# Eight one-bank PSUM tiles, tanh by single banks, and new prices for changes of tile size in a planned attention and MLP kernel

## The chip, the cores and the metric

The kernel runs on one core of a Trainium2 chip. The metric is the device time of one execution in microseconds (us). The engines are named as in the profile: PE (TensorE matmul) and PEld (its weight loads), DVE (VectorE), ACT (ScalarE), POOL (GpSimd) and SP (the queue that issues the DMAs). Each engine works through its own instructions in the order in which the program lists them.

## The reference

Attention with a soft cap, a first MLP with a rational activation, and a second MLP whose hidden layer is a maximum over three products:

```python
scores = cap * np.tanh(scale * np.matmul(q, k.transpose(0, 1, 3, 2)) / cap)   # 2 x 12 heads, 448 x 448
scores = scores - np.max(scores, axis=-1, keepdims=True)
attn = np.exp(scores); attn = attn / (np.sum(attn, axis=-1, keepdims=True) + 1e-09)
x = heads_joined(np.matmul(attn, v))                      # 896 tokens x 768
h = x @ moe_w_in                                          # 896 x 2048
g = (a0 + a1*h + a2*h**2 + a3*h**3) / (1 + |b0|*|h| + |b1|*h**2 + 1e-6)
x2 = g @ moe_w_out                                        # 896 x 768
h3 = np.maximum(np.maximum(x2 @ w1, x2 @ w2), x2 @ w3)
out = h3 @ w_out2                                         # 896 x 768
```

## The kernel before

**A planner writes the order.** Every piece of work is added as an operation with its engines and their prices (`add`). Then `Flow.issue` plays the whole program through with those prices and emits the instructions of every engine in the order in which the play started them. For PE it takes the operation that is due first; but if that one has another tile size (`mode`) than the one before, it looks for one of the same size that is due at most `SAME` = 3.0 us later. A change of tile size costs `SWITCH` = 0.1 us in the play. The prices decide the order and which engine does work that several can do; on the chip nothing waits for them.

**PSUM.** There are eight banks, allocated as four tiles of two banks (`twos`, L315). The planner hands out single banks (`place`): scores ("sc") take both banks of a pair, (0,1) or (2,3), in the first four groups also (6,7); sums of attention ("av") take bank 4 or 5; the products of the first MLP's upper half ("h") take 6 or 7. When all scores are done, any bank goes to "h" and to the six accumulators "acc" of the lower half. `bank(val)` returns half of a tile, `pair(val)` a whole one. The waits between engines are made from the tiles that the instructions read and write.

**Attention** (about the first 95 to 115 us). In six groups of two head pairs, `scores` makes 42 tiles of 128 x 896: two matmuls side by side on half the rows of the array (L515, mode "rows", 36 tiles) or four quarter ones (L522, "both", 6 tiles). ACT then does one tanh over both banks (`soft`, L535) and one exp (L538). `weighted` multiplies with v (L574, "halves"; the rest L555, "both"), `summed` adds up the exponentials (L597, "quarters"). All of them are fp32 and are priced 0.752 us each (`FULL`). The row sums travel through DRAM (L606 to L632).

**First MLP.** `up` makes 32 units of 18 matmuls, in three parts of six (L663, 0.203 us each by plan). Each unit's bank is read by ACT in `cubic` (L683) and `absolute` (L680) and by DVE in `first` (L694) and `second` (L697). DVE and ACT then form the rational function (L702 to L728) and its two parts (`parts`, L742, L745). `down` multiplies those with the output weights into the accumulators (L770), in two halves of the columns. L770 takes its operands from L742, L745 and the weights, not from L680 to L697.

**Second MLP and output.** `branches` makes 36 products of 18 matmuls (L861), DVE and ACT take the maximum and split it into two parts (`H3`, one column range for each half of the tokens). `output` multiplies seven tiles of 128 tokens (L920) and writes them out. In the plan each output waits for both halves of the tokens of all six H3.

The weights arrive as 64-bit floats; DVE, ACT and POOL decode them (L400 to L441) all along the first two thirds.

Of the kernel before, what the change touches and what calls it, by code (L numbers as in the profile page):

```python
# [8 lines left out]
F32 = mybir.dt.float32  # L9
# [3 lines left out]
AF = mybir.ActivationFunctionType  # L13
# [4 lines left out]
B, H, S, D = 2, 12, 448, 64  # L18
P = 128
# [15 lines left out]
NFULL = S // P  # L35
# [6 lines left out]

BACKLOG = 14.0, 2.0

SWITCH, SAME = 0.1, 3.0
MM, MO, FULL = 0.203, 0.1733, 0.752

SHARE = 0.5
# [22 lines left out]
class Flow:  # L71
# [83 lines left out]
    def issue(self):  # L155
# [12 lines left out]
        mode = None  # L168
# [7 lines left out]
        while left:  # L176
# [4 lines left out]
            while moved:  # L181
                moved = False
                for e in names:
                    if busy[e] > t + 1e-9:
                        continue
                    blocked = set()
                    ahead = dict.fromkeys(names, 0.0)
                    choice = None
                    for op in ready:
                        if choice and (op.due > choice.due + SAME or "pe" not in op.engines or op.mode != mode):  # L190
                            continue
                        first = next(iter(op.engines))
                        cost = op.engines[first]
                        if op.ready > t + 1e-9:
                            continue
                        lacking = {v.kind for v in op.vals if v.at is None}
                        if lacking & blocked:
                            continue
                        ok = op.due - v0 < op.ahead and self.fits(op, v0)
                        if not ok:  # L200
                            if op.due - v0 < min(op.ahead, 14.0):
                                blocked |= lacking
                            continue
                        if e not in op.engines:
                            ahead[first] += cost
                            continue
                        if op.shared and e == "dve" and busy["pool"] > t + 1e-9:
                            continue
                        if e == "sp" and op.due - v0 > BACKLOG[0] and wire > t + BACKLOG[1]:
                            continue  # L210
                        if e == "pool" and not self.port(t, op, ready, busy, current, v0):
                            continue
                        if e != first and op.engines[e] > max(0.0, busy[first] - t) + ahead[first] + cost:
                            ahead[first] += cost
                            continue
                        if e == "pe" and SAME and op.mode != mode:
                            choice = choice or op
                            continue
                        choice = op
                        break  # L220
                    if choice is None:
                        continue
                    op = choice
                    ready.remove(op)
                    for v in op.vals:
                        if v.at is None:
                            self.take(v)
                    dur = op.engines[e]
                    if e == "pe":
                        dur += SWITCH if mode != op.mode else 0.0  # L230
                        mode = op.mode
                    op.on = e
                    current[e] = op
                    busy[e] = t + dur
                    if e == "sp":
                        wire = max(wire, t + 1.0) + op.size / 0.28
                        end = max(wire + 0.6, t + 2.5 + op.size / 0.5)
                    else:
                        end = t + dur + self.TAIL[e]
                    op.done = end  # L240
                    op.fn(e)
                    left -= 1
                    self.log.append((t, busy[e], e, op))
                    for x in (busy[e], end):
                        seq += 1
                        heapq.heappush(events, (x, seq, op if x == end else None))
                        if busy[e] == end:
                            break
                    moved = True
                    if e == "pe":  # L250
                        while head < len(order) and order[head].done is not None:
                            head += 1
                        v0 = order[head].due if head < len(order) else self.clock
# [37 lines left out]
def attention_moe(ctx: ExitStack, tc: tile.TileContext, qk, v, w_in, w_out, w123, w_out2, par, out):  # L291
# [20 lines left out]
    ones = cp.tile([P, 3, Q], F32, name="ones")  # L312
    raws = [sp.tile([P, DM, 2], I32, name=f"raw{i}") for i in range(NRAW)]
    rows = [sp.tile([P, S], F32, name=f"row{i}") for i in range(NROW)]
    twos = [pp.tile([P, 2, 512], F32, name=f"b{i}") for i in range(4)]  # L315
    a0, a1, a2, a3 = (con[:, i : i + 1] for i in range(4))
    b0, b1 = absb[:, 0:1], absb[:, 1:2]
    cap = con[:, CAP : CAP + 1]
# [11 lines left out]
    def two(val):  # L330
        return val.tile
# [2 lines left out]
        return two(val).rearrange("p a s -> p (a s)")[:, :n]  # L334

    def bank(val):
        return twos[val.at[0] // 2][:, val.at[0] % 2]

    def pair(val):
        return twos[val.at[0] // 2]  # L340

    def dma(out_, in_, after=(), vals=(), size=0.0, issue=0.4, **kw):
        return add({"sp": issue}, lambda e: nc.sync.dma_start(out=out_(), in_=in_()), after, vals, size=size, **kw)
# [159 lines left out]
    def scores(d, i):  # L503
        whole_ = i < 2 * NFULL
        r, n = divmod(i, NFULL)
        pis = [2 * d + r] if whole_ else [2 * d, 2 * d + 1]
        t, x = Val("sc", f"sc{d}_{i}"), slot(f"e{d}_{i}")
        t.early = d < EARLY

        def products(e):  # L510
            raw = QK[pis[0]][0]
            q, k = two(raw)[:, 0], two(raw)[:, 1, n * P : n * P + P]
            for j in range(2):
                rr = slice(j * D, j * D + D)
                pe.matmul(pair(t)[:, j, :S], k[rr], q[rr], start=True, stop=True)  # L515

        def ends(e):
            for h, pi in enumerate(pis):
                raw = QK[pi][0]
                for j in range(2):  # L520
                    rr = slice(j * D, j * D + D)
                    pe.matmul(  # L522
                        pair(t)[h * D : h * D + D, j, :S], two(raw)[rr, 1, NFULL * P :], two(raw)[rr, 0],
                        start=True, stop=True,
                    )

        done = add(
            {"pe": FULL}, products if whole_ else ends, [QK[pi][1] for pi in pis], [QK[pi][0] for pi in pis] + [t],
            mode="rows" if whole_ else "both",
        )  # L530
        for th in last_tanh[-2:]:
            th.before(done)

        def soft(e):
            act.activation(two(x), pair(t)[:, :, :S], AF.Tanh, scale=qscale)  # L535

        def expo(e):
            act.activation(two(x), two(x), AF.Exp, scale=cap)  # L538

        th = add({"act": 0.89}, soft, [done, scale_in], [t, x])  # L540
        last_tanh.append(th)
        E[d, i] = x, add({"act": 0.935}, expo, [th], [x])

# [360 lines left out]
    def output(t):  # L904
        tk = slice(t * P, t * P + P)
        ob = slot(f"ob{t}")
        last = t == NT // P - 1
        copies = []
        for half in range(2):
            o = Val("h", f"o{t}_{half}")  # L910
            ck = slice(half * NH, half * NH + NH)

            def products(e, o=o, ck=ck):
                terms = []
                for oc in range(NCC):
                    hi, lo = (flat(H3[oc][z], NT)[:, tk] for z in range(2))
                    wh, wl = w_hl(weights["o2", oc])
                    terms += [(hi, wh[:, ck]), (hi, wl[:, ck]), (lo, wh[:, ck])]
                for i, (h_, w_) in enumerate(terms):
                    pe.matmul(bank(o)[:, :NH], h_, w_, start=i == 0, stop=i == len(terms) - 1)  # L920

            ws = [weights["o2", oc] for oc in range(NCC)]
            done = add(
                {"pe": 18 * MO}, products, [w.done for w in ws] + [d for h in H3 for d in h[2]],
                [o] + [x for w in ws for x in (w.hi, w.lo)] + [x for h in H3 for x in h[:2]],
            )
            first = "dve" if half == 0 else "act"
            cost = {"dve": 0.48, "act": 0.38}
            copies.append(add(
                {first: cost.pop(first), **cost},  # L930
                lambda e, o=o, half=half: copy_on[e](two(ob)[:, half, :NH], bank(o)[:, :NH]), [done], [o, ob],
                due=fl.clock,
            ))
            if last:
                dma(lambda ck=ck: out[tk, ck], lambda half=half: two(ob)[:, half, :NH], [copies[-1]], [ob],
                    size=0.2, issue=0.4, due=fl.clock)
# [54 lines left out]
```

## Time and profile before

| what | value |
|---|---|
| median of 3 runs | 537.22 us (536.57 to 540.04) |
| profiled execution | 537.27 us |
| its span, first to last instruction | 535.5 us |
| busy share of the span | PE 96%, PEld 76%, DVE 66%, ACT 56%, POOL 10% |
| mean granted TensorE clock | 0.996 of 2.4 GHz |

The profiled execution lies 0.05 us above the median. A row of the timeline gives start, length, engine, line, operation and count, and in brackets the idle time of the engine before it with the instruction that ended it. Matmuls are pipelined: their recorded lengths overlap the next one's start, so PE is busy in the record for a while after it has nothing left to start.

### The profile page before, as it was taken

Reading aid. Unit: us, or ns where it says so; the run is one execution under the profiler, and the core shown is the slowest. Engines: PE = TensorE matmul, PEld = TensorE weight load, DVE = VectorE, ACT = ScalarE, POOL = GpSimd, SP = SyncE. Lnnn points to the kernel's source line nnn. Section 1 sums busy time; section 2 is a strip of 40 time slices with the busy share of each in tenths; the row PEclk is TensorE's granted clock in tenths of the full one; section 3 lists DMA queues with packets and bytes.
Section 4 is the critical chain, followed back from the end, with each engine's and each line's share of the span. In section 5 each row is a group of like instructions: output and inputs, shape, how many; then the busy total and the mean of one; then the engine's idle time right before and its main releaser. Section 6 shows DMA issues by size and latency. Waiting matters only on the chain.

```text
span 535.5 us, 6669 instructions
## 1 busy us (share of the span) xinstructions
PE 516.2 (96%) x2637; PEld 409.5 (76%) x2637; DVE 354.7 (66%) x485; ACT 299.1 (56%) x376; POOL 51.6 (10%) x46
## 2 busy tenths in 40 slices
PE   8999999889988999999999999999999999999997
PEld 4223223349777989888888799999999999999997
DVE  0268798699789999986789999989964235311000
ACT  6999899567587767665676853556521220101111
POOL 0121201030223212001000200100000000000000
PEclk9999999899999999999999999999999999999999
DMA  8856635533610003300001578666700000000121
GB/s 311 347 183 215 225 118 210 158 94 117 207 67 2 0 1 118 119 1 1 1 1 59 171 239 263 219 229 235 236 0 1 0 2 0 1 0 2 60 82 66
DMA packets 16448, 58.37 MB, mean 109 GB/s; under 512 B 3592, under 2 KB 6944, under 8 KB 16416
## 3 DMA queue, kind: packets, MB, share of 16 engines
q1 hardware_dynamic: 16416, 57.94, 31.5%
q8 instruction: 20, 0.33, 0.3%
q14 instruction: 12, 0.10, 0.1%
HBM read 55.10 MB, written 2.84 MB: 108 GB/s over the span
## 4 chain that ended last, share of the span: by engine, by line
PE 73%; DVE 14%; ACT 6%; DMA 3%; issue 2%; SPq 1%; DVEq 0%; ACTq 0%
PE b L861 25%; PE b L770 17%; PE b L663 10%; PE b L920 8%; PE b L515 5%; PE b L597 3%; PE b L574 3%; DVE W L697 2%; DMA row<-rsum 2%; DVE T L722 1%; ACT A L680 1%; DVE W L694 1%; DVE W L725 1%; ACT W L683 1%; DVE T L702 1%
## 5 line engine op out<-in xcount | busy, mean ns | idle before, releaser
L861 PE MATMUL b<-x,whm 128*128 128x448 f32 x432 | 122.7, 365 | 0.0
L663 PE MATMUL b<-x,whin 128*128 128x448 f32 x384 | 111.5, 372 | 5.2 <-DVE W L697 5.0
L663 PEld LDWEIGHTS b<-x,whin 128*128 128x128 f32 x384 | 71.2, 189 | 21.0 <-DVE W L697 7.3
L861 PEld LDWEIGHTS b<-x,whm 128*128 128x128 f32 x432 | 81.1, 188 | 6.4
L861 PE MATMUL b<-x,wlm 128*128 128x448 f32 x216 | 78.9, 365 | 0.0
L663 PE MATMUL b<-x,wlin 128*128 128x448 f32 x192 | 70.6, 368 | 0.0
L535 ACT ACTIVATE e<-b,qscale 128x896 f32<-128x896 f32 x42 | 41.3, 1023 | 5.3 <-PE b L515 5.0
L861 PEld LDWEIGHTS b<-x,wlm 128*128 128x128 f32 x216 | 40.6, 188 | 3.2
L538 ACT ACTIVATE e<-e,con 128x896 f32<-128x896 f32 x42 | 42.1, 1053 | 0.0
L770 PE MATMUL b<-gh,whoa 128*128 128x448 f32 x96 | 36.5, 380 | 5.3 <-ACT W L683 1.9
L663 PEld LDWEIGHTS b<-x,wlin 128*128 128x128 f32 x192 | 36.2, 189 | 3.1
L889 ACT CAST h3h<-t 128x448 fp32r<-128x448 f32 x11 | 6.2, 567 | 57.2 <-DVE t L884 57.2
L770 PE MATMUL b<-gh,whob 128*128 128x448 f32 x96 | 35.3, 367 | 1.1 <-DVE x L789 1.1
L770 PE MATMUL b<-gl,whoa 128*128 128x448 f32 x96 | 35.2, 367 | 0.9 <-DVE gl L745 0.9
L683 ACT ACTIVATE W<-b,con 128x448 f32<-128x448 f32 x32 | 23.0, 724 | 22.0 <-PE b L663 19.7
L770 PE MATMUL b<-gh,wloa 128*128 128x448 f32 x96 | 35.1, 366 | 0.0
L770 PE MATMUL b<-gh,wlob 128*128 128x448 f32 x96 | 35.1, 365 | 0.0
L770 PE MATMUL b<-gl,whob 128*128 128x448 f32 x96 | 35.0, 365 | 0.0
L515 PE MATMUL b<-qk 64*128 64x448 f32 x144 | 34.4, 577 | 0.0
L422 ACT ACTIVATE raw<-raw 128x768 uint8<-128x768 uint8 x16 | 31.5, 1972 | 2.0 <-POOL deco L402 1.7
L879 DVE TENSOR_TENSOR t<-b,t 128x448 f32<-128x448 f32 x12 | 7.5, 624 | 36.2 <-PE b L861 23.3
L574 PE MATMUL b<-e,v 128*64 128x448 f32 x144 | 29.8, 548 | 0.0
(115 smaller groups left out, 907.1 us busy)
## 6 DMA issues: line engine op xcount, KB each, us to landing
raw<-in_w_out_dram SPq DMA_DIRECT2D x22, 768.0 KB, 4.8
raw<-in_w_dram SPq DMA_DIRECT2D x18, 768.0 KB, 4.6
raw<-in_w_in_dram SPq DMA_DIRECT2D x16, 768.0 KB, 6.6
qk<-in_qk_dram SPq DMA_DIRECT2D x12, 448.0 KB, 7.9
v<-in_v_dram SPq DMA_DIRECT2D x6, 448.0 KB
row<-rsum SPq DMA_DIRECT2D x24, 112.0 KB, 3.1
out_dram<-ob SPq DMA_DIRECT2D x6, 384.0 KB, 2.7
out_dram<-ob SPq DMA_DIRECT2D x2, 192.0 KB, 1.9
```

Source lines behind the costliest of these rows:

```text
L422: act.activation(byte[:, 4::8], byte[:, 3::8], AF.Copy, scale=1 / 32, bias=-31 / 64)
L515: pe.matmul(pair(t)[:, j, :S], k[rr], q[rr], start=True, stop=True)
L535: act.activation(two(x), pair(t)[:, :, :S], AF.Tanh, scale=qscale)
L538: act.activation(two(x), two(x), AF.Exp, scale=cap)
L574: pe.matmul(bank(o)[j * D : j * D + D, :S], whole(vr, n, r, j), two(x)[:, j], start=False, stop=n == NFULL - 1,)
L597: pe.matmul(bank(t)[g, :S], ones[:, 0 if n < NFULL else 1 + r], two(xs[r][0])[:, j], start=n == 0, stop=n == NFULL, tile_position=(0, (2 * ...
L663: pe.matmul(bank(h)[:, :S], w_, x_, start=cc == 0 and i == 0, stop=cc == NCC - 1 and i == len(terms) - 1)
L683: act.activation(two(w_)[:, i], bank(h)[:, :S], AF.Identity, bias=a2, scale=a3)
L697: dve.scalar_tensor_tensor(out=two(w_)[:, i], in0=two(w_)[:, i], scalar=a1, in1=bank(h)[:, :S], op0=ALU.add, op1=ALU.mult)
L770: pe.matmul(bank(a)[:, :S], w_, g_, start=count[half, o, b] == 1, stop=count[half, o, b] == 3 * NFC)
L861: pe.matmul(bank(o)[:, :S], w_, x_, start=cc == 0 and i == 0, stop=cc == NCC - 1 and i == 2)
L920: pe.matmul(bank(o)[:, :NH], h_, w_, start=i == 0, stop=i == len(terms) - 1)
```

## The change

- The four PSUM tiles of two banks become eight tiles of one bank; `bank` and `pair` follow. The planner's choice of banks stays.
- The tanh over two banks becomes two instructions of 448 columns, one for each bank. Its price in the plan goes from 0.89 to 0.87 us for both.
- The price of a change of tile size goes from 0.1 us to one by the new size: 0.21 "rows", 0.16 "both" and "halves", 0.13 "quarters", 0.2 for full size.
- An output waits in the plan for the halves of the tokens that it reads instead of both. Six of seven tiles lie in one half (384 to 511 lies in both).

```diff
-SWITCH, SAME = 0.1, 3.0
+SWITCH, SAME = {"rows": 0.21, "both": 0.16, "halves": 0.16, "quarters": 0.13, None: 0.2}, 3.0
...
-                        dur += SWITCH if mode != op.mode else 0.0
+                        dur += SWITCH[op.mode] if mode != op.mode else 0.0
...
-    twos = [pp.tile([P, 2, 512], F32, name=f"b{i}") for i in range(4)]
+    singles = [pp.tile([P, 512], F32, name=f"b{i}") for i in range(8)]
...
     def bank(val):
-        return twos[val.at[0] // 2][:, val.at[0] % 2]
-
-    def pair(val):
-        return twos[val.at[0] // 2]
+        return singles[val.at[0]]
+
+    def pair(val, j):
+        return singles[val.at[j]]
...
-                pe.matmul(pair(t)[:, j, :S], k[rr], q[rr], start=True, stop=True)
+                pe.matmul(pair(t, j)[:, :S], k[rr], q[rr], start=True, stop=True)
...
         def soft(e):
-            act.activation(two(x), pair(t)[:, :, :S], AF.Tanh, scale=qscale)
+            for j in range(2):
+                act.activation(two(x)[:, j], pair(t, j)[:, :S], AF.Tanh, scale=qscale)
...
-        th = add({"act": 0.89}, soft, [done, scale_in], [t, x])
+        th = add({"act": 0.87}, soft, [done, scale_in], [t, x])
...
+        halves = range(t * P // S, ((t + 1) * P - 1) // S + 1)
...
-                {"pe": 18 * MO}, products, [w.done for w in ws] + [d for h in H3 for d in h[2]],
+                {"pe": 18 * MO}, products, [w.done for w in ws] + [h[2][b] for h in H3 for b in halves],
```

## Rows read from the trace of the kernel before

**Rows 1.** Busy us (instructions) of each engine by stage; then clock, DMA share, GB/s

```profile
5.00:47.00 42.00, 42.00 (x247) 12.11 (x248) 18.76 (x24) 39.98 (x45) 6.03 (x6) 1.00 0.75 290
47.00:95.00 48.00, 46.15 (x278) 15.37 (x276) 40.25 (x63) 44.60 (x50) 6.57 (x7) 1.00 0.57 187
...
95.00:165.00 70.00, 63.54 (x315) 47.18 (x312) 58.88 (x84) 45.93 (x61) 14.82 (x11) 0.98 0.37 118
165.00:301.00 136.00, 130.31 (x624) 115.42 (x622) 120.38 (x154) 94.94 (x128) 17.48 (x10) 1.00 0.12 38
```

**Rows 2.** Pieces of the chain that ended last: start, us, what

```profile
35.41 3.16 PE b L574 x16
...
41.31 0.95 PE b L515 x4
42.27 0.89 PE b L597 x8
...
90.61 1.42 PE b L663 x6
...
356.92 131.33 PE b L861 x648
488.25 43.73 PE b L920 x252
```

**Rows 3.** PE's waits from 90 to 165: total us, times, longest

```profile
PE b L663 <- DVE W L697: 5.0, 3, 2.0
```

**Rows 4.** PE's waits from 165 to 301

```profile
PE b L770 <- ACT W L683: 1.9, 4, 0.8
PE b L770 <- ACT A L680: 1.4, 1, 1.4
PE b L770 <- DVE W L697: 1.2, 2, 0.7
PE b L770 <- DVE W L694: 0.4, 2, 0.2
```

**Rows 5.** Timeline of PE and of ACT around 223 us

```profile
222.47 0.36 PE L770 MATMUL b<-gh,wloa 128*128 128x448 f32 x1
223.67 0.47 PE L770 MATMUL b<-gh,whoa 128*128 128x448 f32 x1 [0.83 <-ACT W L683]
...
222.90 0.72 ACT L683 ACTIVATE W<-b,con 128x448 f32<-128x448 f32 x1
224.58 0.55 ACT L680 ACTIVATE A<-b 128x448 f32<-128x448 f32 x1 [0.97 <-PE b L770]
```

**Rows 6.** Timeline of all engines, 115 to 122 us

```profile
115.63 0.73 ACT L683 ACTIVATE W<-b,con 128x448 f32<-128x448 f32 x1 [4.20 <-PE b L663]
...
117.53 0.37 PE L663 MATMUL b<-x,wlin 128*128 128x448 f32 x1
...
118.01 0.62 DVE L694 TENSOR_TENSOR W<-b,W 128x448 f32<-128x448 f32 x1 [0.52 <-PE b L663]
...
118.66 0.54 ACT L680 ACTIVATE A<-b 128x448 f32<-128x448 f32 x1 [0.58 <-DVE W L694]
...
119.71 0.67 DVE L697 SCALAR_TENSOR_TENSOR W<-W,con,b 128x448 f32<-128x448 f32 x1
...
120.43 0.68 PE L663 MATMUL b<-x,whin 128*128 128x448 f32 x2 [1.64 <-DVE W L697]
```

**Rows 7.** ACT in attention by form, then stretches of ACT's timeline

```profile
L535 ACT ACTIVATE e<-b,qscale 128x896 f32<-128x896 f32 x42 | 41.3, 1023 | 5.3 <-PE b L515 5.0
...
6.17 6.41 ACT L535 ACTIVATE e<-b,qscale 128x896 f32<-128x896 f32 x7 [1.95 <-PE b L515]
...
245.54 1.34 ACT L683 ACTIVATE W<-b,con 128x448 f32<-128x448 f32 x2
...
249.16 0.98 ACT L680 ACTIVATE A<-b 128x448 f32<-128x448 f32 x2 [1.45 <-DVE W L697]
```

**Rows 8.** Waits of ACT and DVE on each other from 165 to 301

```profile
ACT A L718 <- DVE T L702: 8.5, 5, 2.7
...
DVE T L722 <- ACT A L719: 6.3, 4, 2.1
```

More of the change, by code (lines that the diff above doesn't have):

```diff
@@ L522, in ends @@
                     pe.matmul(
-                        pair(t)[h * D : h * D + D, j, :S], two(raw)[rr, 1, NFULL * P :], two(raw)[rr, 0],
+                        pair(t, j)[h * D : h * D + D, :S], two(raw)[rr, 1, NFULL * P :], two(raw)[rr, 0],
                         start=True, stop=True,
```

## The prediction

> **What bounds the kernel now.** I read the busy time by stage first, then the chain that ended last, then PE's waits, then the timeline at single waits.
>
> From 301 us on PE is the bound and has no holes: the chain is one piece of 648 matmuls in 131.33 us (0.203 us each), then 252 of the output in 43.73 us (0.1735 each), with nothing in between [rows 2]. No edit makes a matmul shorter, so these 234 us stay.
>
> In attention, 5 to 95 us, two engines are full at once: PE is busy 42.0 + 46.15 = 88.1 of 90 us and ACT 39.98 + 44.60 = 84.6 of 90 [rows 1]. That PE is the tighter of the two shows in the chain: the pieces of this stage follow each other at 0.89 to 0.95 us [rows 2], with no room for a wait on ACT in them (below).
>
> Between 95 and 301 us PE is busy 63.54 of 70 and 130.31 of 136 us, 12.2 us idle in all, while DVE is at 84% and 89% [rows 1]. Here lies what can be won, and the waits say what ends the idle time. L663 waits 5.0 us in 3 places for L697 [rows 3], L770 waits 1.9 + 1.4 + 1.2 + 0.4 = 4.9 us in 9 places for L683, L680, L697 and L694 [rows 4]. By the code L770 needs nothing that these four make: they read the bank of a unit of `up`, L770 writes an accumulator in another bank.
>
> **Part 1, eight tiles.** One of these waits close by: a matmul of L770 starts at 222.47, the next of the same line only at 223.67, when L683, begun at 222.90, has ended; and L680 behind it, which reads a bank that L663 filled, waits in its turn for L770 [rows 5]. Both make sense only if instructions on the two banks of one tile are kept apart as if they touched the same data. A second place says the same: at 118.01 L694 reads the bank that L683 was already reading at 115.63, so the unit was complete, and still it waits for a later group of L663 that ends at 117.90. At 120.43 the next group of L663 waits for L697 to finish with that bank [rows 6]. So the waits come from the tile, not from the data, and eight tiles remove them.
>
> What they cost: 4.9 us in 9 waits and 5.0 us in 3. The record hides a little of each: a matmul is recorded with 0.36 us [rows 5] but the next starts after 0.203 us [rows 2], so each wait has 0.16 us more that count as busy. 9.9 + 12 x 0.16 = 11.8 us.
>
> Not all of that comes back. If PE gained all 4.9 + 9 x 0.16 = 6.3 us of the later stage, DVE's 120.4 us would have to fit in 129.7 us, 93% instead of 89% [rows 1]. DVE and ACT hand the rational function back and forth there, and lose 8.5 and 6.3 us in waits on each other that are of the data and stay [rows 8]. One of the three waits of L663 may also be for a bank that is truly still in use. Bounds: all of it (11.8 us; no true wait takes the place), and one third (3.9 us; most of them only become a true wait for the same evacuation a little later). I take two thirds, 7.9 us: DVE has idle time in both stages (11 and 16 us), so the middle would be too low, but it is in order and nearly full.
>
> The score matmuls write both banks of a pair; with a tile each they wait for the tanh of their own bank. PE does not wait for tanh in attention now (part 3), so I put this at nothing; if PE comes to wait for ACT, the first bank is free a little earlier and the second a little later than now, which cancels.
>
> **Part 2, tanh by single banks.** Now seven tanh in a row take 6.41 us with a mean length of 1.023 us, so one starts every (6.41 - 1.02) / 6 = 0.90 us [rows 7]. A tanh of 448 columns is not in the trace. The nearest rows are two L683 in a row in 1.34 us (one 0.72, so a step of 0.62; scale and bias both from a tensor) and two L680 in 0.98 us (one 0.55, step 0.43; neither from a tensor) [rows 5, 7]. Tanh has its scale from a tensor and lies between: 0.53 us by the middle. Two are 1.06 us, 0.16 us more than one of 896: 42 x 0.16 = 6.7 us more work for ACT. The bounds by the two rows are 42 x (0.86 - 0.90) = -1.7 us and 42 x (1.24 - 0.90) = +14.3 us; that single pointers cost about half of two makes values far from the middle unlikely. The plan believes 0.87 us and so has ACT about 8 us too early by the end of attention.
>
> The Trainium skill (ScalarE: Activation LUTs, section "What ACT_TABLE_LOAD costs") gives an ACTIVATE 186 ns plus 0.833 ns a column, 93 ns for each pointer operand, and 93 ns of overlap back to back. By that, as an estimate, a half would step by 559 ns and a whole by 932 ns, so a pair costs 0.19 us more and 42 of them 7.8 us; the trace's own 0.90 us for a whole lies a little under it. It speaks against this edit, as the rows do.
>
> ACT has 90 - 84.6 = 5.4 us idle in attention [rows 1], nearly all of it before a tanh (5.0 us); the 1.95 us before the first tanh cannot be filled, because no score exists yet [rows 7]. That leaves 3.5 us of cover. 6.7 - 3.5 = 3.2 us come out at the end of attention, and since PE is full there and in order, PE gets them as waits. Bounds: 1.3 us (all 5.4 us filled) and 6.7 us (none, because the idle time lies in the wrong places).
>
> **Part 3, prices of a tile change.** Nothing runs differently for it; only the order may. Four groups of L574 take 3.16 us, one alone with a change about 0.90, so a group without a change is 0.75 us. A lone L515 takes 0.95, a lone L597 0.89, and six L663 take 1.42 us against 6 x 0.203 = 1.22: changes cost 0.20, 0.14 and 0.20 us [rows 2]. The new table is near this, the old 0.1 us was too low, so PE now runs in the plan as it does on the chip. It also shows that attention's pieces consist of work and changes alone, without waits. What the new order does I cannot read: ten changes more or fewer would be 10 x 0.16 = 1.6 us either way. I take zero.
>
> **Part 4, outputs by halves.** The plan had a wait in front of the first output; the chip has none: L861 ends and L920 begins in one chain without a gap [rows 2]. The products of the first five H3 and the order of the outputs, unchanged, cover it. Zero; bounds zero as well, since there is no idle time to win.
>
> **Sum.** 537.3 (profiled, 0.05 above the median) - 7.9 + 3.2 + 0 + 0 = 532.6 us.
>
> **Rivals.**
> - *All waits go, and attention hides the tanh.* 11.8 won, 1.3 lost: 526.8 us. For it: DVE and ACT have idle time after 95 us. Against it: both engines are full before. Chance 0.23.
> - *True waits take the place of the false ones.* DVE is the bound from 95 to 301 us: 3.9 won, 3.2 lost: 536.6 us. For it: 89% busy and the waits of rows 8; L680 waits for L694 on one and the same bank [rows 6], and such waits stay with eight tiles. The Trainium skill (PSUM — Partial Sum Buffer, section "PSUM bank collisions raise a hardware error") states that two engines must not access one bank at once even where both read; the row agrees with 0.58 us. Chance 0.20.
> - *ACT becomes the bound of attention, slower.* The place is L535 and the price is a tanh pair at 1.06 us and more where the plan says 0.87. If nothing is hidden (6.7 us) or a half steps as L683 does (0.62 us: 14.3 - 3.5 = 10.8 us), and one third is won back: 537.3 + 6.7 - 3.9 = 540.1, or 544.2 us. It decides against the change from where attention loses over 7.9 us. Chance 0.13.
> - *The tiles do nothing*, because waits go by something other than the tile: only the tanh is left, 540.5 us. Against it stand rows 5 and 6. Chance 0.04.
>
> The forecast itself has 0.40, with a range of its own of 530 to 535.5 us.
>
> **How the numbers follow.** About 1% (5.4 us) is what a measurement here can tell from no change; faster by more means below 531.9, slower above 542.6 us. Faster: the first rival (0.23) and a third of the forecast's case, 0.37. Slower: two thirds of the third rival and a part of the fourth, 0.11. Within 1%: 0.52. The range goes from 526.5 (the first rival) to 540.5 us (the third rival's lower value and the fourth) and leaves out about 0.15, mostly above.
>
> **What would show it.** Right, if L770 no longer waits for L680, L683, L694 or L697, if L663's 5.0 us go down, and PE's idle time from 95 to 301 us falls by some 8 us; if L535 has 84 rows that step by about 0.53 us; if ACT's busy time in attention rises by 6 to 7 us and the last exp comes about 3 us later; and if the stages from the second half of `down` on are as long as before. Wrong, if L770 still waits for them (then not the tile), if a half steps by 0.43 or 0.62 us, if the order changes so much that there are clearly more tile changes than now, or if DVE, filled up, holds PE with true waits (L770 on L745, L663 on its own bank).

## The result and the profile after

The changed kernel takes 533.58 us (median of 20 runs, 528.90 to 538.08) against 538.24 us before (20 runs, 535.52 to 540.88): ratio 0.9905, 95% interval 0.9881 to 0.9930. That is about 5 us faster, with 532.6 us forecast; it is clear of no change, and just inside the 1% to which the prediction gave its largest chance. The ratio leaves out two long runs of the changed kernel that count as slow (538.08 and 537.41 us), and the profiled execution (span 536.3 us) is the longer of them. A part of its length is that its 448-column matmuls step 2% slower from 300 us on than in the profile before, 2.6 us in the second MLP alone (last section). Of the 4.7 us between the medians the profiles show less: the second MLP begins at 355.17 us in this one and at 353.92 us in a second one (536.85 us, also a long run), against 356.92 us before. So the profiles show which waits went and which came; no profile shows a run of the median's length.

The busy time by stage after, with the columns of [rows 1]:

```profile
5.00:47.00 42.00, 41.56 (x229) 13.41 (x228) 15.38 (x20) 40.01 (x63) 7.55 (x6) 1.00 0.76 289
47.00:95.00 48.00, 46.37 (x260) 14.99 (x258) 37.31 (x57) 46.13 (x70) 10.83 (x7) 1.00 0.57 182
95.00:165.00 70.00, 66.36 (x340) 48.61 (x337) 66.61 (x93) 46.52 (x64) 15.21 (x13) 0.98 0.43 133
165.00:301.00 136.00, 134.36 (x649) 121.05 (x648) 121.48 (x154) 97.81 (x130) 19.73 (x13) 1.00 0.10 35
```

Between 95 and 301 us PE is idle 5.3 us instead of 12.2 [rows 1], and DVE is now busy 95% of the first of these stages instead of 84%. In attention ACT has 86.1 us in 90 instead of 84.6, and its work runs on past 95 us.

All waits of PE in the execution after (total us, times, longest):

```profile
PE b L771 <- DVE gl L746: 2.9, 2, 2.2
PE b L598 <- DVE xu L583: 1.9, 2, 1.4
PE b L380 <- DVE idle L348: 1.4, 1, 1.4
PE b L515 <- ACT e L536: 1.0, 2, 0.6
PE b L664 <- DVE W L698: 0.7, 2, 0.5
PE b L556 <- ACT row L607: 0.5, 1, 0.5
```

(L771 is L770 of before, L664 is L663, L536 is L535 and so on: the lines have moved by one or two.) The four waits of [rows 4] are gone, and the 5.0 us of [rows 3] are 0.7. What is left for L771 is a wait on `gl`, its own operand, and in attention there are now waits of the scores on the tanh.

The chain that ended last says the same of attention. Start, us, what, in the changed kernel:

```profile
5.10 1.91 PE b L515 x4
7.01 3.24 ACT e L536 x6
10.25 0.93 ACT e L539
11.18 4.20 ACT e L536 x8
...
26.20 3.15 ACT e L536 x6
...
57.25 3.73 ACT e L539 x4
```

Before, the chain was PE's, piece after piece, from the first of these rows to the second:

```profile
5.10 1.77 PE b L515 x8
...
45.95 0.93 PE b L597 x8
```

Now it is ACT's from 7 to 61 us, but for about 1 us. Six halves of tanh in 3.15 us are 0.525 us each. There is no more of a gap ahead of the output than before: the second MLP (L862) ends and the output (L922) begins in one chain.

```profile
355.17 133.92 PE b L862 x648
489.09 43.70 PE b L922 x252
```

### The profile page after: what moved, and what is told of

Read it like the earlier page. It is cut to its first block, busy times and chain, and to the rows that moved or that the text cites. A ratio compares the mean times of both kernels' runs of the same rounds, so it can differ in the third digit from the quotient of the medians.

```text
span 536.3 us, 6729 instructions
## 1 busy us (share of the span) xinstructions
PE 524.1 (98%) x2637; PEld 415.1 (77%) x2637; DVE 354.9 (66%) x480; ACT 302.4 (56%) x418; POOL 57.4 (11%) x51
## 4 chain that ended last, share of the span: by engine, by line
PE 68%; DVE 13%; ACT 10%; DMA 5%; issue 2%; SPq 1%; DVEq 0%; ACTq 0%
PE b L862 25%; PE b L771 19%; PE b L664 15%; PE b L922 8%; ACT e L536 5%; ACT e L539 5%; DMA row<-rsum 3%; DVE W L695 1%; DVE gl L746 1%; SPq L343 1%; DVE W L698 1%; DVE xu L636 1%; DMA comp<-sums 1%; DMA rsum<-comp 1%; DVE wlin L430 1%
## 5 line engine op out<-in xcount | busy, mean ns | idle before, releaser
L862 PE MATMUL b<-x,whm 128*128 128x448 f32 x432 | 124.2, 368 | 0.0
L664 PE MATMUL b<-x,whin 128*128 128x448 f32 x384 | 112.6, 374 | 0.9 <-DVE W L698 0.7
L862 PEld LDWEIGHTS b<-x,whm 128*128 128x128 f32 x432 | 81.1, 188 | 8.2
L664 PEld LDWEIGHTS b<-x,whin 128*128 128x128 f32 x384 | 71.7, 190 | 16.8 <-issue 8.0
L862 PE MATMUL b<-x,wlm 128*128 128x448 f32 x216 | 79.5, 368 | 0.0
L664 PE MATMUL b<-x,wlin 128*128 128x448 f32 x192 | 71.0, 370 | 0.0
L536 ACT ACTIVATE e<-b,qscale 128x448 f32<-128x448 f32 x84 | 51.4, 795 | 3.2 <-PE b L515 3.2
L539 ACT ACTIVATE e<-e,con 128x896 f32<-128x896 f32 x42 | 47.0, 1252 | 0.0
L862 PEld LDWEIGHTS b<-x,wlm 128*128 128x128 f32 x216 | 40.5, 188 | 4.1
L515 PE MATMUL b<-qk 64*128 64x448 f32 x144 | 38.4, 595 | 1.0 <-ACT e L536 1.0
L664 PEld LDWEIGHTS b<-x,wlin 128*128 128x128 f32 x192 | 36.5, 190 | 3.3
L771 PE MATMUL b<-gl,whoa 128*128 128x448 f32 x96 | 35.4, 369 | 2.9 <-DVE gl L746 2.9
L771 PE MATMUL b<-gh,whoa 128*128 128x448 f32 x96 | 35.3, 368 | 0.1
L771 PE MATMUL b<-gh,whob 128*128 128x448 f32 x96 | 35.3, 368 | 0.0
L771 PE MATMUL b<-gl,whob 128*128 128x448 f32 x96 | 35.3, 368 | 0.0
L771 PE MATMUL b<-gh,wlob 128*128 128x448 f32 x96 | 35.3, 368 | 0.0
L771 PE MATMUL b<-gh,wloa 128*128 128x448 f32 x96 | 35.2, 367 | 0.0
L515 PEld LDWEIGHTS b<-qk 64*128 64x128 f32 x144 | 14.3, 192 | 24.7 <-ACT e L536 13.0
L703 POOL TENSOR_TENSOR T<-T,A 128x448 f32<-128x448 f32 x14 | 20.0, 1434 | 99.8 <-ACT T L688 67.8
```

The lines of the kernel that those rows point to most:

```text
L515: pe.matmul(pair(t, j)[:, :S], k[rr], q[rr], start=True, stop=True)
L536: act.activation(two(x)[:, j], pair(t, j)[:, :S], AF.Tanh, scale=qscale)
L664: pe.matmul(bank(h)[:, :S], w_, x_, start=cc == 0 and i == 0, stop=cc == NCC - 1 and i == len(terms) - 1)
L703: engine[e].tensor_tensor(out=two(t_)[:, i], in0=two(t_)[:, i], in1=two(a_)[:, i], op=ALU.mult)
L771: pe.matmul(bank(a)[:, :S], w_, g_, start=count[half, o, b] == 1, stop=count[half, o, b] == 3 * NFC)
L862: pe.matmul(bank(o)[:, :S], w_, x_, start=cc == 0 and i == 0, stop=cc == NCC - 1 and i == 2)
```

## Experiments

Each kernel was timed beside the kernel before on the same chip; a ratio is to that. In the table below, PE's lost time is worked out from the traces: the time since 5.1 us less the work that PE has started by then, at 0.752 us for a group of attention, 0.203 us for a matmul of 448 columns and 0.14 to 0.20 us for a change of tile size. It holds true and false waits, stretches at half the clock, and the 4 ns more of each matmul that steps by 207 ns (last section) alike.

```
PE's lost time, us                            up to 95   95 to 165   165 to 300
before                                           2.6        9.9         9.1
halved tanh alone                                4.9        9.2         8.5
tiles, halved tanh, old prices                   4.5        5.7         3.3
   the same, second profile                      4.9        4.9         2.5
changed kernel                                   8.8        6.6         4.7
   the same, second profile                      8.8        6.4         3.7
changed, old price of a tile change              5.2        3.6         3.7
changed, tanh priced 0.89                        8.1        2.3         2.9
new prices of a tile change alone                4.9        7.2        16.2
```

### The tanh alone, then with the tiles, in the order of before

Theory: the waits that were read as false come from two-bank tiles and are worth 8 us, and the halved tanh costs 3 us. Rivals: the split pays for itself, or the gain is one of the new prices. These two kernels have before's order on PE, DVE, POOL and SP, instruction for instruction; on ACT each tanh is two.

Halved tanh alone:

```diff
-            act.activation(two(x), pair(t)[:, :, :S], AF.Tanh, scale=qscale)
+            for j in range(2):
+                act.activation(two(x)[:, j], pair(t)[:, j, :S], AF.Tanh, scale=qscale)
```

> The kernel before with one edit: the tanh in two halves, its price in the plan left at 0.89 us, so that every engine has the order of before. Theory one (a half steps by 0.53 us, ACT gets 42 x 0.16 = 6.7 us more in attention, 3.5 us of it hidden): 3 to 7 us slower than before, some 541 to 545 us, and L770 waits for L680, L683, L694 and L697 as before (about 5 us in 9 waits). Rival (a half lets PE have the first bank sooner, and that pays for the split): within 1 us of before.

Measured: 540.20 us, ratio 1.0041 (1.0009 to 1.0073): 2.2 us slower by the ratio, under the 3 to 7 us expected. The false waits are all still there (its PE waits, first the longest from 90 to 165 us, then all from 165 to 301 us):

```profile
PE b L664 <- DVE W L698: 5.0, 3, 2.0
...
PE b L771 <- ACT W L684: 1.8, 4, 0.8
PE b L771 <- ACT A L681: 1.3, 1, 1.3
PE b L771 <- DVE W L698: 1.2, 2, 0.7
PE b L771 <- DVE W L695: 0.4, 2, 0.2
```

With the tiles as well:

```diff
-    twos = [pp.tile([P, 2, 512], F32, name=f"b{i}") for i in range(4)]
+    singles = [pp.tile([P, 512], F32, name=f"b{i}") for i in range(8)]
...
-            act.activation(two(x), pair(t)[:, :, :S], AF.Tanh, scale=qscale)
+            for j in range(2):
+                act.activation(two(x)[:, j], pair(t, j)[:, :S], AF.Tanh, scale=qscale)
```

> The kernel before with eight one-bank tiles and the tanh in two halves; prices of before (0.1 us for a change of size, 0.89 us for the tanh), so the order of before on every engine. Theory one (the waits come from the tile): 6 to 10 us faster than the kernel with the halved tanh alone, and 2 to 6 us faster than before (some 532 to 536 us); no wait of L770 for L680, L683, L694 or L697 is left. Rival (the changed kernel gains by the new prices and their order, the tiles are worth little): no faster than before, and the changed kernel stays 4 us or more below it.

Measured: 530.91 us, ratio 0.9849 (0.9808 to 0.9890): 9.3 us below the halved tanh alone, as expected, and about 8 us below before, more than expected. Its PE waits, first from 90 to 165 us, then from 165 to 301 us:

```profile
PE b L771 <- DVE gl L746: 3.6, 1, 3.6
...
PE b L771 <- ACT A L681: 0.6, 1, 0.6
PE b L664 <- DVE W L698: 0.3, 1, 0.3
```

The only difference between the two programs is which data the instructions are taken to share, and with it 9 us go. The tile theory stands; both rivals fall. The table places most of the gain: 3.5 us between 95 and 165 us and 5.2 us from there to 300 us. Not quite all of this line's waits vanish: one of 0.6 us on L681 is left. It stands three matmuls behind the place of the 1.4 us on L680 before [rows 4], where by the plan an accumulator takes over bank 3 from a unit, so it is a true wait in place of the false one. And from 90 to 165 us a true one has grown, L771 on its own operand `gl` (3.6 us, where the halved tanh alone waits 0.8 us).

This kernel is also 2.7 us below the changed one, though the intervals of the two ratios just touch, so the rest of the change seems to cost time. The next runs ask what.

### The prices

The changed kernel with an honest price for the halves:

```diff
-        th = add({"act": 0.87}, soft, [done, scale_in], [t, x])
+        th = add({"act": 1.05}, soft, [done, scale_in], [t, x])
```

> The changed kernel with one edit: the plan prices the two halves of the tanh at 1.05 us instead of 0.87 us, which is what they take in the trace after (six in 3.15 us). Theory one (a plan that is 42 x 0.18 = 7.6 us too early for ACT makes PE wait in attention): 1 to 3 us faster than the changed kernel. Rival (ACT is full in attention whatever the order, so the price changes nothing): within 1 us of it.

Measured: 531.15 us, ratio 0.9836 (0.9784 to 0.9888). The middle is 2.4 us below the changed kernel, but its interval touches that one's, so the 1 to 3 us of its theory one are not shown.

The changed kernel itself beside the next three:

> The changed kernel itself, unedited, beside the next three on one chip, with a second profile of it. Expected 531 to 535 us; in its profile the last exp of attention ends about 3 us later than in the kernel with tiles and halved tanh at the old prices (96.4 us there, 99.5 us in the first profile of the changed kernel).

Measured: 533.57 us, ratio 0.9888 (0.9837 to 0.9939), the same as at first. Its last exp ends at 99.3 us.

Old price for a change of tile size:

```diff
-SWITCH, SAME = {"rows": 0.21, "both": 0.16, "halves": 0.16, "quarters": 0.13, None: 0.2}, 3.0
+SWITCH, SAME = dict.fromkeys(("rows", "both", "halves", "quarters", None), 0.1), 3.0
```

> The changed kernel with one edit: a change of tile size costs 0.1 us in the plan again; the tanh stays at 0.87 us. The kernel with tiles and halved tanh at the old prices (0.1 and 0.89 us) was about 3 us below the changed one. Theory one (the new prices of a change of size give an order in which ACT, full in attention, ends later): 530 to 531.5 us, as that kernel. Rival one (it is the 0.87 us of the tanh): within 1 us of the changed kernel. Rival two (any change of a price shuffles the order and moves the time by a few us without a rule): anywhere from 528 to 536 us.

Measured: 530.25 us, ratio 0.9823 (0.9779 to 0.9867).

The new prices of a tile change, but the tanh at its price of before:

```diff
-        th = add({"act": 0.87}, soft, [done, scale_in], [t, x])
+        th = add({"act": 0.89}, soft, [done, scale_in], [t, x])
```

> The changed kernel with one edit: the plan prices the halved tanh at 0.89 us instead of 0.87 us, with the new prices for changes of size. Theory one (the new prices of a change of size cost the 3 us): within 1 us of the changed kernel. Rival one (the 0.87 us does): 2 to 3 us faster. Rival two (any price shuffles the order): anywhere from 528 to 536 us; since 0.02 us on 42 pieces is 0.8 us of the plan, a move of more than 1.5 us would speak for it.

Measured: 529.86 us, ratio 0.9834 (0.9789 to 0.9878): 3.7 us below the changed kernel on the same chip, for 0.02 us in a price that no instruction knows of. So neither price alone is the cause: taking back either one wins about the same 3 to 4 us. Nor is it the slower step of a matmul in the last section: the profiles of the last two kernels have it too, and still their second MLP begins 5 to 6 us before that of the changed kernel's second profile (353.92 us). The first row is of the old price of a tile change, the second of the tanh at 0.89 us:

```profile
347.60 133.92 PE b L862 x648
```

```profile
348.73 133.92 PE b L862 x648
```

The four neighbours lie together (0.9823 to 0.9849), the changed kernel above them. Theory one of both runs falls; rival two is nearest, with this addition, that the neighbours don't scatter, and the combination of the change is the one that comes out badly.

Then the new prices alone, on the kernel before:

```diff
-SWITCH, SAME = 0.1, 3.0
+SWITCH, SAME = {"rows": 0.21, "both": 0.16, "halves": 0.16, "quarters": 0.13, None: 0.2}, 3.0
...
-                        dur += SWITCH if mode != op.mode else 0.0
+                        dur += SWITCH[op.mode] if mode != op.mode else 0.0
```

> The kernel before with one edit: the new prices for changes of tile size, in the plan alone; tiles of two banks and the whole tanh stay. In attention the kernels with the new prices so far lose 7 to 9 us of PE's time by 95 us, those with the old ones 4.5 to 5. Theory one (the new prices give attention a worse order): 2 to 4 us slower than before, 540 to 542 us. Rival (the order only matters where ACT is full, that is with the halved tanh): within 1.5 us of before.

Measured: 548.61 us, ratio 1.0175 (1.0138 to 1.0212): 9.4 us slower, more than twice what was expected. The table says where most of it lies: 2.3 us in attention, and 7.1 us more than before from 165 to 300 us (less 2.7 us between the two). The rest, some 3 us, comes after 300 us, where PE still waits 2.6 us for L786 and L789. PE's timeline at 165 us:

```profile
164.90 0.52 PE L770 MATMUL b<-gh,whoa 128*128 128x448 f32 x1 [2.50 <-ACT gh L742]
167.05 0.74 PE L770 MATMUL b<-gl,whoa 128*128 128x448 f32 x1 [1.63 <-DVE gl L745]
167.59 0.58 PE L770 MATMUL b<-gh,wloa 128*128 128x448 f32 x1
167.96 0.58 PE L770 MATMUL b<-gh,whoa 128*128 128x448 f32 x1
```

and the busy time (columns as in [rows 1]):

```profile
165.00:172.00 7.00, 5.37 (x14) 4.37 (x15) 5.18 (x7) 5.14 (x8) 0.00 (x0) 0.51 0.01 4
172.00:185.00 13.00, 11.86 (x55) 9.70 (x55) 11.02 (x15) 9.30 (x12) 1.20 (x1) 1.00 0.19 60
```

PE has run out of units and waits for the two parts of the rational function, first `gh`, then `gl`; these are true waits, for its own operands, of an order that puts L770 there too soon. Behind the two waits the granted clock is 0.51, that is the lower level of 1.2 GHz, and a matmul of 448 columns starts every 0.37 us. False waits are left elsewhere, since the tiles are those of before. So the new order is worth +9.4 us with two-bank tiles, and about +3 us with eight tiles at the tanh price of the change, and nothing that can be told at 0.89 us. The parts of this change don't add up.

### Banks 0 to 3 as pairs again

The rest of the edit gives the pair tiles their whole tanh and keeps `acc0` in banks 0 to 5 and the units of `up` in 6 and 7:

```diff
-    singles = [pp.tile([P, 512], F32, name=f"b{i}") for i in range(8)]
+    twos = [pp.tile([P, 2, 512], F32, name=f"t{i}") for i in range(2)]
+    singles = [pp.tile([P, 512], F32, name=f"b{i}") for i in range(4)]
...
-            order = [(4,), (5,)] if v.kind == "av" else [(i,) for i in range(8)]
+            if v.kind == "av":
+                order = [(4,), (5,)]
+            elif v.name[:4] == "acc0":
+                order = [(i,) for i in range(6)]
+            elif v.kind == "h" and v.name[0] == "h":
+                order = [(6,), (7,)]
+            else:
+                order = [(i,) for i in range(8)]
```

> The changed kernel with banks 0 to 3 as two tiles of two banks again and banks 4 to 7 as tiles of one; a score tile in banks 0 to 3 gets one tanh over both, one in banks 6 and 7 two; the planner keeps the first six accumulators in banks 0 to 5 and the units of up in 6 and 7, so that no accumulator shares a tile with a unit; the tanh is priced 0.93 us. Theory one (the gain is from accumulators and units no longer sharing a tile, and the tanh over both banks is cheaper): about three quarters of the 42 tanh go back from 1.05 to 0.90 us, 5 us less for ACT in attention, no waits of L770's line for the units' evacuation: 1 to 4 us faster than the changed kernel. Rival (the planner needs the free choice of banks, and the units wait for their two banks): as slow as the changed kernel or slower.

Measured: 534.72 us, ratio 0.9920 (0.9884 to 0.9956), not faster than the changed kernel. Its two largest waits of PE:

```profile
PE b L611 <- DVE xu L596: 4.3, 3, 2.3
PE b L677 <- DVE W L711: 2.4, 2, 2.1
```

L677 is L663 of before: with two banks alone for the units, it waits for L697's evacuation again, and now truly. The rival holds. ACT is spared (82.8 us busy from 5 to 95 us instead of 86.1), and the time is no better for it. The order is another one too, and the granted clock was lower from 95 to 165 us (0.93, against 0.98 in the changed kernel), so the parts were not told apart:

```profile
95.00:165.00 70.00, 63.65 (x303) 46.52 (x302) 65.45 (x93) 47.08 (x60) 11.91 (x8) 0.93 0.43 143
```

### ACT relieved in attention

Theory: with the halved tanh ACT is the bound of attention, so work taken from it there comes back whole. q is scaled by DVE, and the tanh has no operand from a tensor left:

```diff
-        QK[pi] = raw, dma(lambda: two(raw), lambda: src, vals=[raw], size=0.459, issue=0.45, ahead=NEAR)
+        got = dma(lambda: two(raw), lambda: src, vals=[raw], size=0.459, issue=0.45, ahead=NEAR)
+        def scaled(e):
+            q = two(raw)[:, 0]
+            dve.tensor_scalar(out=q, in0=q, scalar1=qscale, scalar2=None, op0=ALU.mult)
+        QK[pi] = raw, add({"dve": 0.36}, scaled, [got, scale_in], [raw])
...
-                act.activation(two(x)[:, j], pair(t, j)[:, :S], AF.Tanh, scale=qscale)
+                act.activation(two(x)[:, j], pair(t, j)[:, :S], AF.Tanh)
...
-        th = add({"act": 0.87}, soft, [done, scale_in], [t, x])
+        th = add({"act": 0.86}, soft, [done, scale_in], [t, x])
```

> The changed kernel with the scale of the tanh taken out of ACT: DVE multiplies each of the 12 q tiles (448 columns) by it when they have landed, and the tanh has no operand from a tensor left; priced 0.86 us for both halves. Theory one (ACT is the bound of attention now, and a half without a scale from a tensor steps by 0.43 us as L680 does): ACT has 42 x 0.19 = 8 us less to do, attention is bound by PE again, 3 to 6 us faster than the changed kernel (some 528 to 531 us). Rival (attention is not what the time hangs on, or the scaling delays the first scores by as much): within 1 us of the changed kernel.

Measured: 530.62 us, ratio 0.9844 (0.9799 to 0.9890). A half does step by 0.43 us: in ACT's timeline of this kernel two take 0.98 us and eight 3.58, so six more take 2.60 us.

```profile
7.58 0.98 ACT L542 ACTIVATE e<-b 128x448 f32<-128x448 f32 x2 [3.31 <-PE b L521]
...
12.04 3.58 ACT L542 ACTIVATE e<-b 128x448 f32<-128x448 f32 x8
```

It lies 3 us below the changed kernel, but no lower than the neighbours that keep the scale, so the gain can't be put down to ACT. Hence the same with the old price of a tile change, which is a fairer pair to the kernel with tiles and halved tanh:

```diff
-SWITCH, SAME = {"rows": 0.21, "both": 0.16, "halves": 0.16, "quarters": 0.13, None: 0.2}, 3.0
+SWITCH, SAME = dict.fromkeys(("rows", "both", "halves", "quarters", None), 0.1), 3.0
```

> Eight tiles of one bank, the tanh in two halves without an operand from a tensor, q scaled by DVE, and the old price of 0.1 us for a change of size. Theory one (attention is bound by ACT with the halved tanh, and ACT now has 8 us less to do there): 1 to 3 us faster than the kernel with tiles and halved tanh at the old prices, some 528 to 530 us; ACT's busy time from 5 to 95 us falls by 5 us or more and the last exp ends by 94 us. Rival (attention is bound by PE and its order, and what ACT wins is lost at the start, where DVE scales before the first scores): within 1 us of it.

Measured: 531.61 us, ratio 0.9882 (0.9837 to 0.9926), no faster than the kernel with tiles and halved tanh, with the end of the last exp at 97.6 us, not 94. And without scaling the first group's q:

```diff
-        QK[pi] = raw, add({"dve": 0.36}, scaled, [got, scale_in], [raw])
+        QK[pi] = raw, got if pi < 2 else add({"dve": 0.36}, scaled, [got, scale_in], [raw])
...
-                act.activation(two(x)[:, j], pair(t, j)[:, :S], AF.Tanh)
+                act.activation(two(x)[:, j], pair(t, j)[:, :S], AF.Tanh, scale=1.0 if d else qscale)
...
-        th = add({"act": 0.86}, soft, [done, scale_in], [t, x])
+        th = add({"act": 0.86 if d else 1.05}, soft, [done, scale_in], [t, x])
```

> The same, but the first two q tiles are not scaled, and the tanh of the first group keeps its scale from a tensor, so that DVE stands before no score of the first group. Theory one (the scaling before the first scores costs about half a microsecond there): 0.5 to 1 us faster than the kernel that scales all. Rival: the same within 0.5 us, as other waits at the start end later.

Measured: 528.66 us, ratio 0.9812 (0.9770 to 0.9853). Beside them, once more unedited, the kernel with tiles, halved tanh and old prices:

> The kernel with tiles and halved tanh at the prices of before once more, unedited, beside these three on one chip: 529 to 532 us, and a second profile. In the profiles so far the matmuls of 448 columns step by 203 ns from 300 us on in some and by 207 ns in others. If that belongs to the kernel, this one shows 203 ns again; if it belongs to the execution, it may show either.

Measured: 529.39 us, ratio 0.9818 (0.9776 to 0.9861). ACT's busy time in attention, this kernel first, then the one with the late scaling (columns as in [rows 1], ACT is the fourth pair):

```profile
5.00:47.00 42.00, 42.00 (x235) 13.90 (x236) 16.16 (x23) 40.87 (x66) 4.77 (x5) 1.00 0.73 282
47.00:95.00 48.00, 45.84 (x276) 14.76 (x272) 37.41 (x61) 46.21 (x69) 9.22 (x7) 1.00 0.55 178
```

```profile
5.00:47.00 42.00, 41.93 (x240) 12.81 (x240) 19.37 (x32) 40.16 (x68) 5.25 (x6) 1.00 0.74 286
47.00:95.00 48.00, 47.37 (x280) 16.42 (x277) 40.81 (x63) 42.12 (x67) 8.93 (x9) 1.00 0.61 186
```

ACT is busy 4.8 us less, PE loses 2.1 us less up to 95 us (2.8 against 4.9), and the times can't be told apart. So what ACT costs attention is about 2 us, near the 2.2 us of the halved tanh alone, and not the 4.8 us that it was relieved of; the two kernels have different orders, so this is no exact price. The theory falls. A reason at hand is that PE is about as tight as ACT there (89.3 of 90 us busy with the late scaling). Scaling all of q costs more than the late one (531.61 against 528.66), but the two also have different orders, so that the start is the cause was not shown.

The two best versions, this one and the tiles with halved tanh at the old prices, beat the changed kernel by some 4 us; no run tells one from the other.

## Why the prediction was right, point by point

**The bound and the part that can be won.** Right: the gain arose before 300 us. From 300 us on PE has no waits in the changed kernel either; its profile is 2.6 us longer there by the step of the second MLP's matmuls. Attention was read as PE's with ACT close behind; with the halved tanh the chain there is ACT's, and the scores' wait for the tanh, put at nothing, is 1.0 us.

**Eight tiles.** The mechanism is shown: same order, 9.3 us. The term was 7.9 us with bounds of 3.9 and 11.8. The two thirds were a little low: DVE, which was to hold part of it back, was busy 92% of the time from 165 to 301 us in the kernel with tiles and old prices, nearly the 93% that the prediction feared, and PE lost only 3.3 us there. That a true wait takes the place of a false one is seen in L771 on `gl`, at 2.9 us in the changed kernel against 0.9 before. The reading that L770 can't need L680, L683, L694 or L697 was the step that carried it. It has one exception that the prediction left out: the first matmul into a bank that an accumulator takes over from a unit must wait for that unit's last reader (the 0.6 us on L681).

**Halved tanh.** A half was to step by 0.53 us from the middle of two rows; it steps by 0.525. The Trainium skill (ScalarE: Activation LUTs, section "What ACT_TABLE_LOAD costs") gave 0.559, as an estimate, and here the measurement decides. Its 93 ns for an operand from a tensor agrees: 0.525 against 0.43 us without is 95 ns. At 2 x 0.525 - 0.90 = 0.15 us, 42 are 6.3 us. What comes out of it was put at 3.2 us and is 2.2 us: the term is right within its bounds, and more of it was hidden than the 3.5 us allowed for.

**Prices.** This is the step that failed, though the total came out. It was put at zero with 1.6 us either way, from ten changes of tile size more or fewer. The number of changes hardly moved (83 before, 81 after). An order has other costs than changes of size, as the runs showed: with the prices alone 9.4 us, of which 7 us lie seventy and more microseconds behind attention, beginning where L770 stands too early. In the changed kernel it is about 3 us. PE loses 4 us more in its attention than with the old prices (8.8 against 4.5 and 4.9 us), but that alone does not explain it: with the tanh at 0.89 us PE loses 8.1 us there and the kernel is as fast as the others, because it loses less behind (2.3 and 2.9 us against 6.6 and 4.7). The new prices are nearer to the 0.14 to 0.20 us that a change costs in the trace, and the order that comes from them is not better. Which of the moved pieces is at fault was not settled.

**Outputs by halves.** Zero as forecast, by the chain of after. It wasn't tried alone on the chip. In the plan, without it the order of PE, POOL and SP is the same, and one cast of some 0.5 us moves from ACT to DVE.

**The sum.** -7.9 + 3.2 + 0 = -4.7 us was forecast; the parts are about -9.3 + 2.2 + 3 = -4.1 us, and -4.7 us by the medians of the 20 runs. So the total came out closer than its terms, and that is luck: a gain that was too small and a loss that was left out cancel. Of the rivals, that ACT becomes the bound of attention is what the chain shows, but at 2 us and not 7 to 11; true waits in place of false ones took a smaller part than feared.

**What was to be seen.** Of the listed signs, the waits of L770 and L663 and the step of 0.53 us came as said; PE's idle time from 95 to 301 us fell by 6.9 us instead of 8. ACT's busy time from 5 to 95 us rose by 1.5 us and not by 6 to 7, as its work ran on past 95 us. One sign of being wrong showed as well, L770 on L745, at a small size (2.9 us). The last exp ended 5.5 us later instead of 3 (99.5 against 94.0 us); the halved tanh alone accounts for 2.3 us (96.3 us), the rest is the order.

## What to carry to other kernels

An instruction that waits for one whose result it doesn't use, on another part of the same tile, is a false wait: sum such rows, add what the record hides as busy time, and split the tile; with this kernel 9.3 of 11.8 us came back. An edit that changes only a planner's prices can move the time by more than the prices say: bound it by what other orders of the same work cost, not by the item that it prices, and time it alone and with its partners, since 0.02 us in one price moved the whole by 3.7 us. Where two engines are both full, relieving one of them of 5 us need not show in the time at all.

## What the runs showed of the hardware

**Two steps of the same matmul.** A matmul of 448 columns at the full clock steps by 203 ns in some stretches and by 207 ns in others. The second MLP, in the changed kernel, its second profile, and the kernel with tiles and old prices:

```profile
355.17 133.92 PE b L862 x648
```

```profile
353.92 133.92 PE b L862 x648
```

```profile
347.92 131.33 PE b L862 x648
```

133.92 / 648 is 0.2067 us, 131.33 / 648 is 0.2027 us, as before [rows 2], and from 300 us on each trace keeps to one. That is 2.6 us in this stage alone. The output's matmuls of 384 columns take 43.7 us in all of them. Between 200 and 220 us the two profiles of the changed kernel, the same program, differ (207 and 203 ns), so the program alone does not decide; the kernel with tiles and old prices showed 203 ns from 300 us on twice, the changed kernel 207 ns twice, and what decides was not found. That it is a part of the scatter between runs of one kernel is likely and was not shown. It does not tell a good kernel from a bad one: the one with the late scaling (528.66 us) has 207 ns from 300 us on too.

**The clock after a stall.** In the profile before the granted clock was 0.50 for 3.4 us from 100.6 us, in the changed kernel for 3.4 us from 144.0 us, and in the kernel with the new prices alone for most of the 7 us shown above. The first two:

```profile
100.60:104.00 3.40, 3.40 (x14) 1.36 (x13) 2.91 (x6) 1.10 (x2) 0.00 (x0) 0.50 0.52 203
```

```profile
144.00:147.40 3.40, 3.40 (x10) 3.03 (x10) 3.37 (x4) 0.00 (x0) 0.63 (x1) 0.50 0.11 28
```

Each time PE had waited shortly before: 2.0 us up to 99.55, 2.2 us up to 143.11, and 2.5 and 1.6 us up to 164.90 and 167.05 us. At the lower clock a matmul steps by 0.37 instead of 0.20 us, so nine of them in 3.4 us lose about 1.5 us: such a wait cost nearly as much again behind it as it took. Not every wait of this length does. Behind the 1.64 us before 120.43 [rows 6], and behind one of 3.0 us in the second profile of the kernel with tiles and old prices, the clock stayed full.
